# A decode block with adaptive layernorm, cached attention and a feed-forward layer: constant matmuls in the tail, and the last V tile ahead of the output weight

## The chip, the cores and the metric

The kernel runs on one core of one Trainium2 chip. The metric is the device time of one execution in microseconds; three plain runs of the kernel before gave 1332.01 to 1332.98 us, with a median of 1332.43.

## The reference

Four sequences decode one token each. D is 512, there are 32 heads of 128, the cache holds 4096 keys and values per head, all in f32 (k_cache and v_cache are 268 MB each).

```python
mod = (_silu(c) @ w_mod).reshape(c.shape[0], 6, 1, -1)
sa, ca, ga, sb, cb, gb = (mod[:, i] for i in range(6))
h = _layernorm(x) * (1 + ca) + sa
q = (h @ wq).reshape(B, Sq, H, Dh).transpose(0, 2, 1, 3)
p = softmax(einsum("bhqd,bhkd->bhqk", q, k_cache) * Dh ** -0.5)
o = einsum("bhqk,bhkd->bhqd", p, v_cache)
x = x + ga * (o.transpose(0, 2, 1, 3).reshape(B, Sq, H * Dh) @ wo)
h = _layernorm(x) * (1 + cb) + sb
x = x + gb * (_silu(h @ w1) @ w2)
```

## The kernel before

The attention is cut into N = 64 steps, one for each pair of heads (t, 16 of them) and sequence (b, 4). A step has a K tile and a V tile of 4 MiB each, 128 partitions of 32 KB. All large tiles (the modulation weights, wq, the K and V tiles, then the two halves of wo, w1 and w2) share one pool, `kv`, of five buffers: a load starts when the tile that had its buffer has been read for the last time. All these loads are issued by SyncE (SP in the profile), in the order of the program, and move in that order.

In a step, GpSimd multiplies 24 of the 64 rows of the K tile by the query, and VectorE the other 40 (`mult`, line 216); VectorE sums the products (`red`, 221) and takes each partition's maximum (`rowmax`, 225). TensorE transposes the maxima (`bmax`, 229), VectorE reduces them (`negmax`, 236), ScalarE computes the exponentials into a zero-padded tile (`softexp`, 247), and TensorE multiplies these with V in 16 matmuls of 512 columns (`pv`, 260), each against 32 columns of weights, so that four column groups work side by side. In f32 each matmul is two records in the trace.

Behind the four steps of a pair t, `finish_a` copies the accumulated rows and sums them with small matmuls (lines 269 to 277), and `finish_b` scales them into `oz`. `project(lo, hi)` (294) multiplies pairs lo to hi of `oz` with wo, 8 matmuls of 128 columns for each pair, into one accumulator, `accp`. The first half of wo (`wo0`) serves pairs 0 to 7, the second (`wo1`, in four pieces) pairs 8 to 15.

The tail, behind step 63, is one chain: `finish_a` and `finish_b` of the last pair, `project(NH, NT)`, the residual (345, 346), the second layernorm with two one-column matmuls (165, 169), a transpose, w1 (352, 16 matmuls of 448 columns in four groups k), SiLU (126, 127), a transpose, w2 (362, 56 matmuls of 128 columns), the last residual and four small stores. `project(0, NH)` stands on TensorE ahead of pv(63).

Scheduling is by hand: each engine runs its instructions in the order in which the program writes them. `psum("q", 2)` hands out two PSUM banks in turn, which make_qb (202) and, at the end, w1's product use. `qs` holds the scaled queries and `ident` the identity matrix; both stay unchanged to the end.

Of the kernel before, what the change touches and what calls it, by code (L numbers as in the profile page):

```python
# [17 lines left out]
def kernel(  # L18
# [13 lines left out]
    nc = tc.nc  # L32
    P = 128
    B, H, S, Dh = kc.shape
    D = x.shape[2]
# [3 lines left out]
    HP = 2  # L39
    HALF = P // HP  # L40
    NT = H // HP
# [4 lines left out]
    NI = F // P  # L46
# [4 lines left out]
    N = B * NT  # L51
# [8 lines left out]
    def psum(shape, tag, bufs):  # L60
        return ps.tile(shape, F32, tag=tag, name=tag, bufs=bufs)
# [3 lines left out]
    wov = wo.rearrange("(t p j) n -> p t j n", p=P, j=HP)  # L65
    w1v = w1.rearrange("(p k) f -> p k f", p=P)
    w2v = w2.rearrange("(p i) d -> p i d", p=P)

    def fetch(t, src, *cuts):
        for lo, hi in zip(cuts, cuts[1:]):  # L70
            nc.sync.dma_start(t[:, lo:hi], src[:, lo:hi])

    def load(name, shape, src, *cuts):
        t = kv.tile(shape, F32, tag="kv", name=name)
        fetch(t, src, *(cuts or (0, shape[1])))
        return t
# [3 lines left out]
    def load_k(n):  # L80
        t, b = divmod(n, B)
        src = kc[b, HP * t : HP * (t + 1)].rearrange("h (p j) d -> (h p) j d", p=HALF)
        kt[n] = load(f"k{n}", [P, NJ, Dh], src)

    def load_v(n):
        t, b = divmod(n, B)
        src = vc[b, HP * t : HP * (t + 1)].rearrange("h (p j) d -> (h p) j d", p=HALF)
        vt[n] = load(f"v{n}", [P, NJ, Dh], src)
# [14 lines left out]
    ident = const.tile([P, P], F32, name="ident")  # L103
# [25 lines left out]
    def transposed(src, m, name):  # L129
        d = const.tile([P, m, W], F32, name=name)  # L130
        nc.vector.transpose(d, src.rearrange("p (c k) -> p k c", k=m))  # L131
        return d
# [23 lines left out]
    def layernorm_mod(dst, src, sh, sc1):  # L156
        def t(tag, n):
            return work.tile([P, n], F32, tag=tag, name=tag, bufs=1)

        st, mv, dm, q, r, u = t("st", 6), t("mv", 2), t("dm", 1), t("lnq", 1), t("lnr", 2), t("lnu", P)  # L160
        nc.vector.bn_stats(st, src)
        nc.vector.bn_aggr(mv, st)
        avgm = avg.rearrange("p g w -> p (g w)")
        pm = psum([P, 1], "mx", 2)
        nc.tensor.matmul(pm, avgm, mv[:, 0:1], start=True, stop=True)
        nc.vector.tensor_sub(dm, mv[:, 0:1], pm)
        nc.vector.scalar_tensor_tensor(q, dm, dm, mv[:, 1:2], op0=ALU.mult, op1=ALU.add)
        pq = psum([P, 1], "mx", 2)
        nc.tensor.matmul(pq, avgm, q, start=True, stop=True)
        nc.vector.scalar_tensor_tensor(u, src, pm, sc1, op0=ALU.subtract, op1=ALU.mult)  # L170
        nc.scalar.activation(r[:, 0:1], pq, AF.Sqrt, bias=epst)
        nc.vector.reciprocal(r[:, 1:2], r[:, 0:1])
        nc.vector.scalar_tensor_tensor(dst, u, r[:, 1:2], sh, op0=ALU.mult, op1=ALU.add)
# [7 lines left out]
    CW = 4 * Dh  # L181
    pq = [psum([P, CW], "q", 2) for _ in range(2)]
    for k in range(NK):
        for ch in range(H * Dh // CW):
# [3 lines left out]
                start=k == 0, stop=k == NK - 1,  # L188
            )
    qs = const.tile([P, 2, CW], F32, name="qs")  # L190
# [5 lines left out]
    def make_qb(t):  # L196
        p = psum([P, B, Dh], "q", 2)
        for b in range(B):
            for i in range(HP):
                ch, u = divmod(HP * t + i, CW // Dh)  # L200
                j, g = divmod(ch, G)
                nc.tensor.matmul(  # L202
                    p[HALF * i : HALF * (i + 1), b, :],
                    ident[:, W * g + b : W * g + b + 1].to_broadcast([P, HALF]),
                    qs[:, j, u * Dh : (u + 1) * Dh],
                    start=True, stop=True,
                )
        qb[t] = p
        qw[t] = work.tile([P, B, Dh], F32, tag="qw", name=f"qw{t}")
        nc.scalar.activation(qw[t], p, AF.Copy)  # L210
# [3 lines left out]
    def mult(eng, src, n, lo, hi):  # L214
        t, b = divmod(n, B)
        eng.tensor_mul(  # L216
            kt[n][:, lo:hi, :], kt[n][:, lo:hi, :], src[t][:, b : b + 1, :].to_broadcast([P, hi - lo, Dh])
        )

    def red(n, lo, hi):  # L220
        nc.vector.tensor_reduce(sc[n][:, lo:hi], kt[n][:, lo:hi, :], axis=AX.X, op=ALU.add)  # L221

    def rowmax(n):
        nm[n] = work.tile([P, 1], F32, tag="rm", name=f"rm{n}", bufs=3)
        nc.vector.tensor_reduce(nm[n], sc[n], axis=AX.X, op=ALU.max)  # L225

    def bmax(n):
        p = psum([P, P], "mx", 2)
        nc.tensor.transpose(p, nm[n].to_broadcast([P, P]), ident)  # L229
        nm[n] = p  # L230

    def negmax(n):
        t = work.tile([P, 1], F32, tag="nm", name=f"nm{n}", bufs=3)
        for i in range(HP):
            h = slice(HALF * i, HALF * (i + 1))
            nc.vector.tensor_reduce(t[h], nm[n][h, h], axis=AX.X, op=ALU.max, negate=True)  # L236
        nm[n] = t
# [29 lines left out]
    def finish_a(t):  # L267
        o = work.tile([P, JJ, Dh], F32, tag="o", name="o")
        nc.vector.tensor_copy(o, po[t].rearrange("p (j d) -> p j d", j=JJ))  # L269
        d = psum([P, 1 + HP, B], "small", 1)  # L270
        nc.tensor.matmul(d[:, 0, :], blk, rs[t], start=True, stop=True)
        for i in range(HP):
            for r in range(HP):
                for j in range(JJ):
                    s = i * W // 2 + j
                    nc.tensor.matmul(  # L276
                        d[HALF * i : HALF * (i + 1), 1 + r, :], o[:, j, r::HP], sel[:, s : s + JJ * (B - 1) + 1 : JJ],
                        start=j == 0, stop=j == JJ - 1,
                    )
        sm[t] = d  # L280

    def finish_b(t):
        rd = work.tile([P, 1, B], F32, tag="rd", name="rd")
        nc.vector.reciprocal(rd, sm[t][:, 0:1, :])
        nc.vector.tensor_mul(oz[:, t, :, :B], sm[t][:, 1 : 1 + HP, :], rd.to_broadcast([P, HP, B]))  # L285

    accp = psum([P, P], "acc", 1)
    wot = []

    def project(lo, hi):  # L290
        for t in range(lo, hi):
            for r in range(HP):
                for g in range(G):
                    nc.tensor.matmul(  # L294
                        accp[W * g : W * (g + 1), :], oz[:, t, r, :],
                        wot[t // NH][:, t % NH, r, g * P : (g + 1) * P],
                        start=(t == 0 and r == 0), stop=(t == NT - 1 and r == HP - 1),
                    )

    NH = NT // 2  # L300
    make_qb(0)
    load_v(0)
    for n in range(N):
        t, b = divmod(n, B)
        if n + 1 < N - 3:
            load_k(n + 1)
            load_v(n + 1)
        elif n == N - 4:
            load_k(N - 3)
            load_k(N - 2)  # L310
            load_k(N - 1)
        elif n == N - 3:
            load_v(N - 3)
            load_v(N - 2)
        elif n == N - 2:
            wot.append(load("wo0", [P, NH, HP, D], wov[:, :NH]))
        else:
            load_v(n)
            wot.append(load("wo1", [P, NH, HP, D], wov[:, NH:], 0, NH // 2, 3 * NH // 4, NH - 1, NH))
        sc[n] = work.tile([P, NJ], F32, tag="sc", name=f"sc{n}", bufs=3)  # L320
        mult(nc.gpsimd, qw, n, 0, NA)
        mult(nc.vector, qb, n, NA, NJ)
        if n >= B and b == 0:
            finish_a(t - 1)
        red(n, NA, NJ)
        if n >= B and b == 0:
            finish_b(t - 1)
        red(n, 0, NA)
        rowmax(n)
        bmax(n)  # L330
        negmax(n)
        softexp(n)
        if n == N - 1:
            w1t = load("w1", [P, NK, F], w1v, 0, 2, 3, 4)
            w2t = load("w2", [P, NI, D], w2v, 0, 8, 12, 13, 14)
            project(0, NH)
        pv(n)
        if b == 1 and t + 1 < NT:
            make_qb(t + 1)
    finish_a(NT - 1)  # L340
    finish_b(NT - 1)
    project(NH, NT)

    x1 = const.tile([P, P], F32, name="x1")
    nc.vector.tensor_mul(x1, ga, accp)
    nc.vector.tensor_add(x1, x1, xg)
    layernorm_mod(hg, x1, sb, cb1)
    h2T = transposed(hg, NK, "h2T")
    ph = psum([P, FG], "q", 2)
    for k in range(NK):  # L350
        for g in range(G):
            nc.tensor.matmul(  # L352
                ph[W * g : W * (g + 1), :], h2T[:, k, :], w1t[:, k, g * FG : (g + 1) * FG],
                start=k == 0, stop=k == NK - 1,
            )
    hid = const.tile([P, FG], F32, name="hid")
    silu2(hid, ph, FG)
    hidT = transposed(hid, NI, "hidT")
    pf = psum([P, P], "po", 2)
    for i in range(NI):  # L360
        for g in range(G):
            nc.tensor.matmul(  # L362
                pf[W * g : W * (g + 1), :], hidT[:, i, :], w2t[:, i, g * P : (g + 1) * P],
                start=i == 0, stop=i == NI - 1,
# [32 lines left out]
```

## Time and profile before

| What | Value |
|---|---|
| Median of three plain runs | 1332.43 us |
| The profiled execution, in all | 1334.54 us |
| Its span, from the first to the last instruction | 1332.5 us |
| VectorE busy | 976.2 us (73%) |
| TensorE matmuls busy | 504.9 us (38%) |
| GpSimd, ScalarE busy | 435.2, 75.7 us |
| Bytes read from HBM | 567.30 MB, 426 GB/s over the span |
| Granted TensorE clock, mean | 0.656 of 2.4 GHz |

The DMA engines are busy to nine tenths or more in 39 of the span's 40 slices; no engine is. Busy shares are over the whole span, and say little about its last 4%, where the loads run out and the engines wait for each other. There the rows of the section below are read. The granted clock of a stretch is a mean of two levels, 0.5 (1.2 GHz) and 1.0 (2.4 GHz).

### The profile page before, as it was taken

Reading aid. Unit: us, or ns where it says so; the run is one execution under the profiler, and the core shown is the slowest. Engines: PE = TensorE matmul, PEld = TensorE weight load, DVE = VectorE, ACT = ScalarE, POOL = GpSimd, SP = SyncE. Lnnn points to the kernel's source line nnn. Section 1 sums busy time; section 2 is a strip of 40 time slices with the busy share of each in tenths; the row PEclk is TensorE's granted clock in tenths of the full one; section 3 lists DMA queues with packets and bytes.
Section 4 is the critical chain, followed back from the end, with each engine's and each line's share of the span. In section 5 each row is a group of like instructions: output and inputs, shape, how many; then the busy total and the mean of one; then the engine's idle time right before and its main releaser. Section 6 shows DMA issues by size and latency. Waiting matters only on the chain.

```text
span 1332.5 us, 8833 instructions
## 1 busy us (share of the span) xinstructions
PE 504.9 (38%) x3576; PEld 181.2 (14%) x3576; DVE 976.2 (73%) x468; ACT 75.7 (6%) x289; POOL 435.2 (33%) x79
## 2 busy tenths in 40 slices
PE   3244324433442533443343233334333333433157
PEld 2011101110110111101011110101111011101024
DVE  1487787788778778777877877777787787778851
ACT  1100000000000000000000000000000000000000
POOL 1244234324323423432442343243234234324600
PEclk9666677666656666656666676576666556666677
DMA  9999999999999999999999999999999999999997
GB/s 407 427 430 433 426 436 428 429 435 426 433 432 429 433 427 435 430 430 432 427 435 429 428 434 429 432 430 431 432 429 430 430 432 432 431 428 433 431 414 288
DMA packets 22376, 567.87 MB, mean 426 GB/s; under 512 B 2448, under 2 KB 2496, under 8 KB 5056
## 3 DMA queue, kind: packets, MB, share of 16 engines
q1 hardware_dynamic: 22160, 567.29, 99.3%
q8 instruction: 28, 0.46, 0.1%
q14 instruction: 12, 0.10, 0.0%
q0 software_dynamic: 128, 0.01, 0.0%
q10 hardware_dynamic: 48, 0.01, 0.0%
HBM read 567.30 MB, written 0.01 MB: 426 GB/s over the span
## 4 chain that ended last, share of the span: by engine, by line
DMA 48%; DVE 35%; PE 10%; issue 4%; ACT 2%; DVEq 0%; ACTq 0%
DMA k<-in_A_k_cache_dram 45%; DVE sc L221 20%; DVE k L216 13%; PE po L260 8%; DMA v<-in_A_v_cache_dram 2%; ACT pz L247 2%; PE mx L229 1%; DMA wm<-in_w_mod_dram 1%; DVE o L269 1%; DVE rm L225 1%; DVE nm L236 1%; PE acc L294 0%; PE po L362 0%; PE q L352 0%; DVE oz L285 0%
## 5 line engine op out<-in xcount | busy, mean ns | idle before, releaser
L216 POOL TENSOR_TENSOR k<-k,qw 128x3072 f32<-128x3072 f32 x64 | 429.7, 6715 | 827.9 <-DMA k<-in_A_k_cache_dram 786.7
L221 DVE TENSOR_REDUCE sc<-k 128x40 f32<-128x5120 f32 (+1 forms) x128 | 560.8, 4413 | 5.2
L216 DVE TENSOR_TENSOR k<-k,q 128x5120 f32<-128x5120 f32 x64 | 351.2, 5488 | 245.9 <-DMA k<-in_A_k_cache_dram 188.2
L260 PE MATMUL po<-v,pz 128*32 128x512 f32 x2048 | 371.5, 892 | 103.0 <-ACT pz L247 77.1
L229 PE MATMUL mx<-ident,rm 128*128 128x128 f32 x64 | 28.5, 445 | 641.4 <-DVE rm L225 641.4
L260 PEld LDWEIGHTS po<-v,pz 128*32 128x32 f32 x2048 | 82.6, 155 | 349.0 <-issue 256.3
L247 ACT ACTIVATE pz<-sc,nm 64x64 f32<-64x64 f32 x128 | 44.2, 345 | 1054.1 <-DVE nm L236 1052.5
L229 PEld LDWEIGHTS mx<-ident,rm 128*128 128x128 f32 x64 | 11.6, 181 | 676.2 <-issue 648.2
L236 DVE TENSOR_REDUCE nm<-mx 64x1 f32<-64x64 f32 x128 | 28.4, 222 | 45.9 <-PE mx L229 43.9
L276 PE MATMUL small<-sel,o 128*64 128x4 f32 x512 | 43.0, 231 | 46.6 <-DVE o L269 46.6
L276 PEld LDWEIGHTS small<-sel,o 128*64 128x64 f32 x512 | 41.6, 190 | 48.0 <-DVE o L269 48.0
L247 ACT ACTIVATION_READ_ACCUMULATOR pz<-sc,nm 64x1 f32 x128 | 23.6, 185 | 0.0
L269 DVE COPY o<-po 128x512 f32<-128x512 f32 x16 | 11.0, 684 | 16.2 <-PE po L260 16.2
L202 PE MATMUL q<-qs,ident 128*64 128x128 f32 x256 | 17.5, 279 | 0.0
L225 DVE TENSOR_REDUCE rm<-sc 128x1 f32<-128x64 f32 x64 | 14.1, 220 | 2.2
L202 PEld LDWEIGHTS q<-qs,ident 128*64 128x64 f32 x256 | 13.6, 136 | 14.5 <-issue 14.5
L210 ACT ACTIVATE qw<-q 128x512 f32<-128x512 f32 x16 | 9.6, 597 | 105.5 <-PE q L202 105.5
L146 PE MATMUL q<-wm,csT 128*32 128x128 f32 x192 | 7.5, 322 | 17.2 <-DVE csT L131 13.5
L186 PE MATMUL q<-wq,hT 128*32 128x512 f32 x64 | 10.1, 790 | 9.5 <-DMA wq<-in_A_wq_dram 9.5
L294 PE MATMUL acc<-wo,oz 128*32 128x128 f32 x256 | 11.7, 369 | 0.4 <-DMA wo<-in_A_wo_dram 0.4
L294 PEld LDWEIGHTS acc<-wo,oz 128*32 128x32 f32 x256 | 11.2, 154 | 0.7 <-issue 0.6
L146 PEld LDWEIGHTS q<-wm,csT 128*32 128x32 f32 x192 | 6.2, 129 | 17.9 <-DVE csT L131 13.5
(57 smaller groups left out, 63.8 us busy)
## 6 DMA issues: line engine op xcount, KB each, us to landing
k<-in_A_k_cache_dram SPq DMA_DIRECT2D x64, 4096.0 KB, 36.0
v<-in_A_v_cache_dram SPq DMA_DIRECT2D x64, 4096.0 KB, 30.3
wq<-in_A_wq_dram SPq DMA_DIRECT2D x2, 4096.0 KB
wm<-in_w_mod_dram SPq DMA_DIRECT2D x2, 3072.0 KB, 10.1
wo<-in_A_wo_dram SPq DMA_DIRECT2D x1, 4096.0 KB
wo<-in_A_wo_dram SPq DMA_DIRECT2D x1, 2048.0 KB
w<-in_B_w_dram SPq DMA_DIRECT2D x1, 2048.0 KB, 23.7
w<-in_B_w_dram SPq DMA_DIRECT2D x1, 1792.0 KB
```

What stands on the lines that cost most here:

```text
L146: nc.tensor.matmul(p[W * g : W * (g + 1), u, :], csT[:, k, :], wmt[k // 2][:, k % 2, o : o + P], start=k == 0, stop=k == NK - 1,)
L202: nc.tensor.matmul(p[HALF * i : HALF * (i + 1), b, :], ident[:, W * g + b : W * g + b + 1].to_broadcast([P, HALF]), qs[:, j, u * Dh : (u + ...
L216: eng.tensor_mul(kt[n][:, lo:hi, :], kt[n][:, lo:hi, :], src[t][:, b : b + 1, :].to_broadcast([P, hi - lo, Dh]))
L221: nc.vector.tensor_reduce(sc[n][:, lo:hi], kt[n][:, lo:hi, :], axis=AX.X, op=ALU.add)
L225: nc.vector.tensor_reduce(nm[n], sc[n], axis=AX.X, op=ALU.max)
L229: nc.tensor.transpose(p, nm[n].to_broadcast([P, P]), ident)
L236: nc.vector.tensor_reduce(t[h], nm[n][h, h], axis=AX.X, op=ALU.max, negate=True)
L247: nc.scalar.activation(w[:, :, o + i * W // 2 : o + i * W // 2 + JJ], sc[n][h].rearrange("p (g j) -> p g j", j=JJ), AF.Exp, bias=nm[n][h], ...
L260: nc.tensor.matmul(po[t][W * g : W * (g + 1), :], pz[n % NP][:, j * W + o : (j + 1) * W + o], vt[n][:, JJ * j : JJ * (j + 1), :].rearrange ...
L269: nc.vector.tensor_copy(o, po[t].rearrange("p (j d) -> p j d", j=JJ))
L276: nc.tensor.matmul(d[HALF * i : HALF * (i + 1), 1 + r, :], o[:, j, r::HP], sel[:, s : s + JJ * (B - 1) + 1 : JJ], start=j == 0, stop=j == ...
L294: nc.tensor.matmul(accp[W * g : W * (g + 1), :], oz[:, t, r, :], wot[t // NH][:, t % NH, r, g * P : (g + 1) * P], start=(t == 0 and r == 0 ...
```

## The change

`busy(m)` issues m matmuls of a constant: the identity against the first 512 columns of `qs`, into a PSUM bank that nothing reads. It is called at seven places: ten matmuls ahead of the transpose of step 63's maxima, five ahead of the second half of the projection, and 2, 3, 2, 2 and 4 in the tail, 28 in all. The V tile of step 63 is loaded ahead of wo0, which comes in two pieces; w2 comes in five pieces where it came in four. `project(0, NH)` moves behind pv(63), in two halves with `finish_a` between them, and pairs 8 to 14 are projected ahead of the last one.

```diff
+    idle = []
+
+    def busy(m):
+        if not idle:
+            idle.append(psum([P, CW], "q", 2))
+        for _ in range(m):
+            nc.tensor.matmul(idle[0], ident, qs[:, 0, :], start=True, stop=True)
+
     make_qb(0)
...
         elif n == N - 2:
-            wot.append(load("wo0", [P, NH, HP, D], wov[:, :NH]))
+            load_v(N - 1)
+            wot.append(load("wo0", [P, NH, HP, D], wov[:, :NH], 0, NH // 2, NH))
         else:
-            load_v(n)
             wot.append(load("wo1", [P, NH, HP, D], wov[:, NH:], 0, NH // 2, 3 * NH // 4, NH - 1, NH))
+            busy(10)
...
         if n == N - 1:
             w1t = load("w1", [P, NK, F], w1v, 0, 2, 3, 4)
-            w2t = load("w2", [P, NI, D], w2v, 0, 8, 12, 13, 14)
-            project(0, NH)
+            w2t = load("w2", [P, NI, D], w2v, 0, 4, 8, 11, 13, 14)
         pv(n)
         if b == 1 and t + 1 < NT:
             make_qb(t + 1)
+    project(0, NH // 2)
     finish_a(NT - 1)
+    project(NH // 2, NH)
+    busy(5)
+    project(NH, NT - 1)
     finish_b(NT - 1)
-    project(NH, NT)
+    project(NT - 1, NT)
...
     nc.vector.tensor_add(x1, x1, xg)
+    busy(2)
     layernorm_mod(hg, x1, sb, cb1)
     h2T = transposed(hg, NK, "h2T")
+    busy(3)
     ph = psum([P, FG], "q", 2)
...
                 start=k == 0, stop=k == NK - 1,
             )
+        if k in (1, 2):
+            busy(2)
+    busy(4)
     hid = const.tile([P, FG], F32, name="hid")
```

On TensorE, from pv(62) on to the first matmuls of the projection behind the last sums over heads (L229 is the transpose of step 63's maxima, L260 pv, L294 the projection, L271 and L276 the sums, L307 the constant):

```order
 L260 MATMUL po<-v_2922,pz_113 32x512 x16
-L229 MATMUL mx<-ident,rm_2998 128x128
-L294 MATMUL acc<-wo_2954,oz 32x128 x64
-L260 MATMUL po<-v_2986,pz_111 32x512 x16
+L307 MATMUL q<-qs,ident 128x512 x10
+L229 MATMUL mx<-ident,rm_3010 128x128
+L260 MATMUL po<-v_2954,pz_111 32x512 x16
+L294 MATMUL acc<-wo_2956,oz 32x128 x32
 L271 MATMUL small<-rs_2900,blk 128x4
 L276 MATMUL small<-sel,o 64x4 x16
-L294 MATMUL acc<-wo_2988,oz 32x128 x64
+L294 MATMUL acc<-wo_2956,oz 32x128 x32
```

The first half of the projection went from ahead of pv(63) to behind it, around the sums, and ten constants stand ahead of the transpose.

On TensorE, from the layernorm's second matmul (L169) to w2 (w1 is L352 before and L366 now, w2 L362 and L379):

```order
 L169 MATMUL mx<-lnq,avg 128x1
-L352 MATMUL q<-w_3007,h2T 32x448 x16
-L362 MATMUL po<-w_3011,hidT 32x128 x56
-L393 UNCONDITIONAL_BRANCH
+L307 MATMUL q<-qs,ident 128x512 x3
+L366 MATMUL q<-w_3019,h2T 32x448 x8
+L307 MATMUL q<-qs,ident 128x512 x2
+L366 MATMUL q<-w_3019,h2T 32x448 x4
+L307 MATMUL q<-qs,ident 128x512 x2
+L366 MATMUL q<-w_3019,h2T 32x448 x4
+L307 MATMUL q<-qs,ident 128x512 x4
+L379 MATMUL po<-w_3023,hidT 32x128 x56
```

w1's sixteen matmuls are parted by two pairs of constants, with three ahead of them and four behind.

On SyncE, the loads behind K of step 63, before (v_2920, v_2922 and v_2986 are the V tiles of steps 61 to 63, wo_2954 and wo_2988 are wo0 and wo1):

```order
L71 DMA v_2920<-in_A_v_cache_dram 128x8192
L71 DMA v_2922<-in_A_v_cache_dram 128x8192
L71 DMA wo_2954<-in_A_wo_dram 128x8x1024
L71 DMA v_2986<-in_A_v_cache_dram 128x8192
L71 DMA wo_2988<-in_A_wo_dram 128x4x1024
```

and now (v_2954 is step 63's, wo_2956 and wo_2989 are wo0 and wo1):

```order
L71 DMA v_2920<-in_A_v_cache_dram 128x8192
L71 DMA v_2922<-in_A_v_cache_dram 128x8192
L71 DMA v_2954<-in_A_v_cache_dram 128x8192
L71 DMA wo_2956<-in_A_wo_dram 128x4x1024 x2
L71 DMA wo_2989<-in_A_wo_dram 128x4x1024
```

The V tile of step 63 went one load forward, and wo0 is two loads.

## Rows read from the trace of the kernel before

**Rows 1.** Chain that ended last, from 1260 us: start us, us, what.

```profile
1267.96 30.29 DMA v<-in_A_v_cache_dram
...
1298.39 6.58 PE po L260 x32
...
1305.74 1.88 PE small L276 x32
1307.62 5.34 PE acc L294 x128
...
1314.29 0.37 PE mx L165 x2
...
1315.24 0.37 PE mx L169 x2
...
1316.96 4.96 PE q L352 x32
...
1324.16 4.97 PE po L362 x112
```

**Rows 2.** Timeline of SyncE's queue, single issues: start us, us, engine line op, count.

```profile
1252.23 0.39 SPq L71 DMA_DIRECT2D wo<-in_A_wo_dram  x1
...
1298.32 0.86 SPq L71 DMA_DIRECT2D w<-in_B_w_dram  x1
...
1303.37 0.33 SPq L71 DMA_DIRECT2D w<-in_B_w_dram  x1
...
1305.91 1.60 SPq L71 DMA_DIRECT2D w<-in_B_w_dram  x2
```

**Rows 3.** Timeline of TensorE: a step's pv, then steps 62 and 63 [idle before].

```profile
1235.64 5.49 PE L260 MATMUL po<-v,pz 128*32 128x512 f32 x32 [1.30 <-ACT pz L247]
...
1276.88 5.34 PE L260 MATMUL po<-v,pz 128*32 128x512 f32 x32 [4.38 <-DMA v<-in_A_v_cache_dram]
...
1287.79 0.44 PE L229 MATMUL mx<-ident,rm 128*128 128x128 f32 x1 [5.57 <-DVE rm L225]
...
1288.60 6.33 PE L294 MATMUL acc<-wo,oz 128*32 128x128 f32 x128 [0.37 <-DMA wo<-in_A_wo_dram]
```

**Rows 4.** Windows: from:to, us, PE busy, granted clock, DMA share, GB/s.

```profile
1280.44:1287.26 6.82, 1.78 (x19) 1.00 1.07 437
...
1297.50:1304.33 6.83, 5.94 (x29) 0.50 1.03 413
1304.33:1307.74 3.41, 2.91 (x50) 0.99 1.03 426
1307.74:1311.16 3.42, 3.42 (x72) 0.51 1.00 417
1311.16:1317.98 6.82, 3.48 (x80) 1.00 1.02 424
1317.98:1321.40 3.42, 3.42 (x24) 0.51 0.74 306
...
1324.81:1328.22 3.41, 3.41 (x72) 0.51 0.04 12
```

**Rows 5.** Weight loads and make_qb's matmuls, from the timeline, then two groups of loads.

```profile
1280.72 0.16 PEld L260 LDWEIGHTS po<-v,pz 128*32 128x32 f32 x4 [0.27 <-issue]
1281.15 0.16 PEld L260 LDWEIGHTS po<-v,pz 128*32 128x32 f32 x4 [0.27 <-issue]
...
1300.07 0.23 PEld L260 LDWEIGHTS po<-v,pz 128*32 128x32 f32 x4 [0.62 <-issue]
1300.92 0.23 PEld L260 LDWEIGHTS po<-v,pz 128*32 128x32 f32 x4 [0.62 <-issue]
...
1182.51 1.09 PE L202 MATMUL q<-qs,ident 128*64 128x128 f32 x16
...
L202 PEld LDWEIGHTS q<-qs,ident 128*64 128x64 f32 x256 | 13.6, 136 | 14.5 <-issue 14.5
L229 PEld LDWEIGHTS mx<-ident,rm 128*128 128x128 f32 x64 | 11.6, 181 | 676.2 <-issue 648.2
```

## The prediction

> **What bounds the kernel now.** I read the chain of waits first, because the change touches only the last 50 us. In that stretch the chain stands on one transfer and then on TensorE: v63 is issued at 1267.96 us and lands after 30.29 us, its matmuls take 6.58 us, then come the sums over heads (1.88), the second half of the output projection (5.34), the layernorm with two tiny matmuls, w1 (4.96 from 1316.96) and w2 (4.97 from 1324.16, so until 1329.13) [rows 1]. Next the DMA queue's own rows: a load is issued there when its buffer and its semaphore are free, so the four issues from 1298.32 on are also landing times: v63 at 1298.3, then the pieces of wo1 at 1303.4, 1305.9 and about 1307.2 (the last of the two rows that begin at 1305.91) [rows 2]. That is 2, 1 and 0.5 MiB in 5.05, 2.54 and about 1.3 us: 2.53 us a MiB, all the time. By that rate the last piece of wo1 lands at 1308.5, w1 (1.75, 0.875, 0.875 MiB) at 1312.9, 1315.1 and 1317.3, and w2 (3.5 MiB) at 1326.1. Nothing of this moves with the change: the same bytes stand in the same queue, only v63 and wo0 change places. So the reader should see two limits close together: w2's last landing, 1326.1, and TensorE's end, 1329.1. Last I read windows cut where the granted clock changes: TensorE works in long stretches at the lower level (1.2 GHz, share 0.5) in the tail: 1297.50 to 1304.33, 1307.74 to 1311.16, 1317.98 to 1321.40 and 1324.81 to 1328.22; it rises only behind a stretch of dense matmuls, and falls behind idle ones [rows 4].
>
> **v63 ahead of wo0.** In the kernel before, wo0 takes the buffer that k61 leaves at 1252.23 and v63 follows when k62 is done [rows 1, 2]. Now v63 has the first place. pv(62) starts on v62's landing at 1276.88 [rows 3]; 4 MiB at 2.53 us is 10.1, so v63 lands near 1287 instead of 1298.3, and wo0 (in halves) near 1292 and 1298. No issue gets later: the extra pieces wait for landings that come well before the queue reaches them.
>
> **The constant's price.** The trace has no such matmul. One is 128x512 in f32 against a full 128-column weight and should be two records, as each of the kernel's other f32 matmuls. The nearest rows are pv's: four column groups stream 512 columns side by side, and the next round's weights are loaded 0.85 us after the last at the lower level and 0.43 at the upper one (2.4 GHz) [rows 5]. So one constant matmul is 2 x 0.427 = 0.85 us at the upper level, 1.71 at the lower. The bound above adds its weight loads, if no stream hides them: 181 ns each in the row of a 128-wide load. I take them as hidden: make_qb's 16 records, eight in each half of the columns, take 1.09 us with loads of 136 ns, where loads in the open would make it 8 x (0.107 + 0.136) = 1.9 [rows 5]. The Trainium skill speaks against it: "TensorE: Matmul & The Clock Gate", Part 3, section "The mechanism", says that a weight load overlaps matmuls in flight only in another row group, and the constant always has all rows. make_qb's loads have all rows too and overlap, so this trace doesn't bear the rule out; by it each constant matmul would cost 0.36 us more.
>
> **The sum.** At the upper level throughout, I rescale each burst by the stretches it lay in (time at the lower level, plus twice that at the upper, halved) [rows 1, 4]: pv 5.94 low + 0.64 high gives 3.6; project's 64 matmuls 3.42 low + 1.92 high gives 3.6; w1 3.42 + 1.54 gives 3.25; w2 3.41 + 1.57 gives 3.3. Now step by step:
> - pv(62) ends at 1282.2, at the upper level since 1280.44 [rows 3, 4]. Ten constants, 8.5 us, until 1290.8. They lie in TensorE's wait for the row maximum, which was over at 1287.79 [rows 3]: the transpose behind them is 3 us late, and so are the exponentials. That would matter if v63 were not also early. Transpose 0.35, then 1.30 for maximum and exponentials [rows 3]: pv(63) starts at 1292.4, 6.0 earlier than before; v63 has landed. It ends at 1296.0.
> - project(0, 4) 1.8 (before, all of project(0, 8) lay hidden in the wait for v63, 6.33 us from 1288.60 [rows 3]; it is now on the path), which hides the copy of po; sums over heads 2.2 with the denominators; project(4, 8) 1.8: 1301.8. Five constants 4.3: 1306.1. They delay little, since the last of wo1 lands at 1308.5. project(8, 15) 3.2, project(15, 16) 0.45: the accumulator is ready at 1309.7, where it was 1312.96. So far -3.2 us.
> - Two constants (1.7) against the wait for the statistics (1312.96 to 1314.29, 1.33) [rows 1]: 0.4 late. The two tiny matmuls 1.3: 1312.75. Three constants (2.6) against the rest of the layernorm (1315.61 to 1316.96, 1.35): 1.2 late, w1 starts at 1315.3.
> - w1 3.25, with four constants between its parts, 3.4: it ends at 1322.0, as before (1321.92). Without them it would have waited for w1's last landing at 1317.3 and ended near 1318.5: the constants take this gain.
> - Four constants (3.4) against SiLU and transpose (1321.92 to 1324.16, 2.24): 1.2 late, w2 starts at 1325.4. At the upper level it takes 3.3 instead of 4.97: 1328.65, where it was 1329.13.
> The sum is -3.2 + 0.4 + 1.2 - 1.7 + 3.4 + 1.2 - 1.7, about **-0.5 us**. VectorE's last steps and the stores stay as they are. Against the profiled execution's own 1334.54 us that is 1334.0; the plain runs have a median of 1332.43, 2.1 lower, so I forecast 1331.9.
>
> What hides what: the five constants lie under wo1's landings; if wo1 came sooner they would cost 4.3. All later ones lie partly open, and pay only because the clock stays up: the upper level is worth 3.4 us on w1 and w2 together, and the constants behind the accumulator cost about 6.2.
>
> **The rivals.**
> 1. The constants are hidden and the transfers bound. Floor: w2's last piece at 1326.1 and four matmuls, 0.2: -2.8 us, 1329.6. For it: everything up to the accumulator runs into landings. Against: 13 constants stand behind it, 11 us of TensorE in 18. Chance 0.08. More than this can't be won while the queue is full.
> 2. The clock falls all the same, somewhere from pv(63) to w2, since small matmuls and waits stand between the constants. One such stretch in the tail lasts 3.4 to 6.8 us [rows 4], and each us in it at the lower level gives half a us back: 1.7 to 3.4 us, 1333.6 to 1335.3. For it: the copy and the sums over heads took the clock down before (up from 1304.33, low at 1307.74, with 1.88 us of 4-column matmuls) [rows 1, 4]. Against: dense matmuls now stand right before and behind. One long stretch decides for slower; a short one does not. Chance 0.10. If a constant didn't raise the clock at all, all 18 behind pv(63) would cost twice as much, 15 us more; that is within this chance, at 0.01.
> 3. The weight loads lie open. Then 56 loads (28 constants of two records) at 0.136 to 0.181 us [rows 5] add 7.6 to 10.1 us, less 1 that wo1's landings cover: 1338.5 to 1341. It turns to slower from 0.06 us a load on. Against: make_qb. Chance 0.04.
> 4. My own: no change that can be told, chance 0.78. Inside it lies the case that before differs from its profile: that execution had four low stretches in the tail, others may have fewer, and a change that repairs the clock then gains nothing and costs up to 1 us.
>
> **How the numbers follow.** I count 0.2%, 2.7 us, as what can be told from no change. Rival 1 ends at -2.8, on that line, so half of it is faster, and a few hundredths I keep for landings other than worked out: faster 0.08. Slower: rival 3 and two thirds of rival 2, 0.11. Same: 0.81. The range goes down to rival 1 (1329.6) and up into the short end of rival 2 (1334.2); it leaves out the long low stretch and rival 3.
>
> **What would show it.** Right: v63's matmuls start on ScalarE's exponentials, not on a DMA, near 1292.4; the L307 records start 0.43 us apart at the upper level; the accumulator is ready near 1309.7 with waits for wo1 gone or short; granted clock 1.0 from 1294 on; w1 ends near 1322 and w2 takes 3.3 us from behind the last constant. Wrong: records 0.56 us or more apart (rival 3), a stretch at 0.5 behind pv(63) (rival 2), w2 waiting for its DMA (rival 1), or transfers that end at another time than 1326.

## The result: 0.23% slower, and the profile after

Nine runs of the changed kernel, the profiled one among them, have a median of 1335.66 us (1334.57 to 1336.62); nine of the kernel before, 1332.51 (1331.86 to 1333.43). The ratio is 1.0023, 95% interval 1.0014 to 1.0032: 3.15 us slower, where I forecast 0.5 us faster and a range up to 1334.2. The profiled execution took 1336.26 us, with a span of 1334.4.

The chain of waits of the changed kernel, from step 62's matmuls on (start us, us, what; lines 307, 366 and 379 are the constant, w1 and w2):

```profile
1276.79 6.40 PE po L260 x32
1283.18 8.78 PE q L307 x20
1291.96 0.12 PE mx L229
...
1293.38 3.64 PE po L260 x32
1297.02 1.75 PE acc L294 x64
...
1299.08 1.81 PE small L276 x32
1300.89 1.88 PE acc L294 x64
1302.77 4.49 PE q L307 x10
1307.26 3.63 PE acc L294 x128
1310.89 1.91 PE q L307 x4
...
1313.51 0.35 PE mx L169 x2
1313.87 2.68 PE q L307 x6
1316.55 1.64 PE q L366 x16
1318.19 1.91 PE q L307 x4
1320.10 0.89 PE q L366 x8
1320.99 1.91 PE q L307 x4
1322.91 0.89 PE q L366 x8
1323.80 3.63 PE q L307 x8
1327.43 3.24 PE po L379 x112
```

From 1276.79 on no transfer is in this chain: each piece of TensorE's work ends where the next begins, but for the steps at 1292 and 1313 that VectorE and ScalarE take. Before, the same stretch began with a wait for v63 until 1298.3 [rows 1]. Now pv(63) starts at 1293.38, 5 us earlier, and w2 still ends 1.5 us later than in the first profile of before: 1330.67 against 1329.13.

The windows of the changed kernel on TensorE (from:to, us, PE busy, granted clock, DMA share, GB/s) answer to [rows 4]:

```profile
1290.00:1300.00 10.00, 8.70 (x124) 1.00 1.03 411
1300.00:1310.00 10.00, 10.00 (x196) 1.00 1.02 418
1310.00:1320.00 10.00, 9.41 (x69) 1.00 0.99 404
1320.00:1330.70 10.70, 10.62 (x141) 1.00 0.24 97
```

The constants do what they can do: the clock stands at the upper level (2.4 GHz) in every window to the end, where before it fell four times. In the last three, 30.7 us, TensorE idles for 0.7. The transfers end in the last window; its DMA share is 0.24. Their times are those worked out: the SyncE queue's issues behind wo1's landings, single rows of the timeline, stand at

```profile
1302.91 0.33 SPq L71 DMA_DIRECT2D w<-in_B_w_dram  x1
1305.53 0.33 SPq L71 DMA_DIRECT2D w<-in_B_w_dram  x1
1306.81 0.33 SPq L71 DMA_DIRECT2D w<-in_B_w_dram  x1
1308.08 0.33 SPq L71 DMA_DIRECT2D w<-in_B_w_dram  x1
```

which is within half a microsecond of before [rows 2]. The projection's second half began at 1307.26, so the five constants ahead of it covered wo1 almost to the end, as the sum had it. They cover more than that: the accumulator is ready at 1310.89, where in traces below that wait for wo1 it is ready at 1308.8 (twice the constants in w1) and 1309.2 (none at all).

### The profile page after: what moved, and what is told of

Read it like the earlier page. It is cut to its first block, busy times and chain, and to the rows that moved or that the text cites. A ratio compares the mean times of both kernels' runs of the same rounds, so it can differ in the third digit from the quotient of the medians.

```text
span 1334.4 us, 8947 instructions
## 1 busy us (share of the span) xinstructions
PE 520.8 (39%) x3632; PEld 185.3 (14%) x3632; DVE 976.2 (73%) x468; ACT 75.7 (6%) x289; POOL 435.1 (33%) x79
## 4 chain that ended last, share of the span: by engine, by line
DMA 46%; DVE 35%; PE 12%; issue 5%; ACT 2%; DVEq 0%; ACTq 0%
DMA k<-in_A_k_cache_dram 43%; DVE sc L221 20%; DVE k L216 13%; PE po L260 8%; DMA v<-in_A_v_cache_dram 3%; ACT pz L247 2%; PE q L307 2%; PE mx L229 1%; DMA wm<-in_w_mod_dram 1%; DVE o L269 1%; PE acc L294 1%; DVE rm L225 1%; DVE nm L236 1%; PE q L366 0%; PE po L379 0%
## 5 line engine op out<-in xcount | busy, mean ns | idle before, releaser
L260 PE MATMUL po<-v,pz 128*32 128x512 f32 x2048 | 369.3, 887 | 99.8 <-ACT pz L247 78.4
L229 PE MATMUL mx<-ident,rm 128*128 128x128 f32 x64 | 28.3, 443 | 638.2 <-DVE rm L225 638.2
L260 PEld LDWEIGHTS po<-v,pz 128*32 128x32 f32 x2048 | 82.0, 155 | 344.8 <-issue 250.2
L229 PEld LDWEIGHTS mx<-ident,rm 128*128 128x128 f32 x64 | 11.5, 180 | 672.4 <-issue 643.6
L276 PE MATMUL small<-sel,o 128*64 128x4 f32 x512 | 42.3, 230 | 46.8 <-DVE o L269 46.8
L276 PEld LDWEIGHTS small<-sel,o 128*64 128x64 f32 x512 | 40.9, 187 | 48.1 <-DVE o L269 48.1
L307 PE MATMUL q<-qs,ident 128*128 128x512 f32 x56 | 25.9, 605 | 0.0
L202 PE MATMUL q<-qs,ident 128*64 128x128 f32 x256 | 17.5, 279 | 0.0
L307 PEld LDWEIGHTS q<-qs,ident 128*128 128x128 f32 x56 | 10.1, 190 | 13.6 <-issue 13.6
```

The costliest lines, as they stand in the source:

```text
L202: nc.tensor.matmul(p[HALF * i : HALF * (i + 1), b, :], ident[:, W * g + b : W * g + b + 1].to_broadcast([P, HALF]), qs[:, j, u * Dh : (u + ...
L260: nc.tensor.matmul(po[t][W * g : W * (g + 1), :], pz[n % NP][:, j * W + o : (j + 1) * W + o], vt[n][:, JJ * j : JJ * (j + 1), :].rearrange ...
L276: nc.tensor.matmul(d[HALF * i : HALF * (i + 1), 1 + r, :], o[:, j, r::HP], sel[:, s : s + JJ * (B - 1) + 1 : JJ], start=j == 0, stop=j == ...
L307: nc.tensor.matmul(idle[0], ident, qs[:, 0, :], start=True, stop=True)
```

## The experiments

Theory A: behind pv(63) the changed kernel is bound by TensorE, which is at the upper level anyhow, and the 18 constants there cost more than the level gives back; without them the transfers bound. Its rivals: B, the lower level would take the same time without constants; C, the new order is what costs; D, the constants in w1 are hidden; and for the part of the price that the sum did not have, S and E below.

**No constants.** The calls of `busy` go, all else stays.

```diff
-            busy(10)
...
-    busy(5)
...
-        if k in (1, 2):
-            busy(2)
-    busy(4)
```

> The changed kernel without any of its 28 constants: v63 still ahead of wo0, the projection still in its new order. Theory A (behind pv(63) the changed kernel is bound by TensorE at the upper level without a gap, and the 18 constants there cost more than the clock pays back): TensorE waits again for wo1 (last piece near 1308) and w2 (near 1326), the end of w2's matmuls goes from 1330.7 to 1326 or 1327, so 3.5 to 4.5 us less than the changed kernel: 1331.1 to 1332.2 us. Rival B (without constants the lower level takes the same time back): 1334 or more, with w1 and w2 at the lower level on the path. Rival C (the new order of loads and of the projection is what costs): 1335 or more, whatever the clock does.

Measured: 1332.03 us (1331.77 to 1332.17, 11 runs), ratio to before 0.9993 (0.9984 to 1.0002). 3.6 us less than the changed kernel, as A said; B and C fall. Its chain:

```profile
1288.25 20.16 DMA wo<-in_A_wo_dram
1308.55 0.68 PE acc L294 x16
...
1313.22 5.96 PE q L354 x32
...
1321.44 4.98 PE po L364 x112
```

The transfers are back in it: the accumulator ends on wo1's last piece, at 1309.2, 1.7 us earlier than with constants. w1 then runs almost wholly and w2 mostly at the lower level (5.96 and 4.98 us), and w2 still ends at 1326.4. The windows of this run, columns as above:

```profile
1310.00:1320.00 10.00, 6.62 (x36) 0.66 0.98 404
1320.00:1326.40 6.40, 4.94 (x112) 0.73 0.41 162
```

TensorE is busy for 4.94 of w2's 4.98 us, so w2 itself does not wait for a transfer here. But its last piece, issued at 1308.43, lands 17.5 us later, at 1325.9: the upper level has at most half a us left to win. Where w2 does run at it, in the kernel without constants inside w1 below, it waits for its landings and ends at 1326.49.

**Constants only.** The kernel before, with the same constants at the same places:

```diff
+            busy(10)
...
     finish_a(NT - 1)
+    busy(5)
     finish_b(NT - 1)
     project(NH, NT)
```

and the calls in the tail as in the change.

> The kernel before with the constants alone: the loads, their pieces and the projection as before; 10, 5, 2, 3, 2, 2 and 4 constants at the same places of the program. Theory A: pv(63) waits for v63 until 1298.4; then pv 3.6, sums 3.0, five constants 4.5 and the second half of the projection 3.7 make the accumulator ready at 1313.1, and from there the tail of the changed kernel takes 19.8 us: 2.2 us later than it, 1337 to 1339 us. Rival C (the order costs, the constants are about free): 1331 to 1333.

Measured: 1339.45 us (5 runs, 1337.79 to 1342.35), ratio 1.0054 (1.0041 to 1.0068): slower than either, against C. It is a little over the range of A, since in the profiled execution step 63's matmuls, behind a wait for v63, took 5.37 us and not 3.6:

```profile
1268.01 30.02 DMA v<-in_A_v_cache_dram
...
1298.17 5.37 PE po L260 x32
...
1310.67 3.63 PE acc L294 x128
1314.31 1.91 PE q L307 x4
```

So the two parts of the change go opposite ways: with the constants, the early v63 and the moved projection save 3.8 us (1339.45 to 1335.66); without them they save what noise covers.

**No constants behind the projection.** The first 15 stay, the 13 of the tail go:

```diff
-    busy(2)
...
-    busy(3)
...
-        if k in (1, 2):
-            busy(2)
-    busy(4)
```

> The changed kernel with its first 15 constants (10 ahead of the transpose, 5 ahead of the projection's second half) and without the 13 behind the projection. Theory A: the accumulator is ready at 1310.9 as in the changed kernel; layernorm 4, w1 behind its last landing (1317.1) near 1318, w2 bound by its own landings, 1326: 3.5 to 4.5 us less than the changed kernel, 1331.1 to 1332.2, the same as without any constant. Rival B: the level falls in the layernorm and w1 and w2 give 2 to 3 us back: 1333.5 to 1335.

Measured: 1332.21 us (11 runs), ratio 0.9997 (0.9988 to 1.0006). The median is A's. But the profiled execution took 1334.13, and there the windows of TensorE show the low stretches that B speaks of:

```profile
1313.70:1320.50 6.80, 5.43 (x30) 0.50 0.96 390
1320.50:1323.90 3.40, 1.09 (x24) 1.00 0.57 231
1323.90:1327.30 3.40, 3.40 (x72) 0.50 0.11 41
```

Almost all of w1 and most of w2 lay at 0.50. One other run of the eleven was at 1333.91, the rest between 1331.97 and 1332.54. The lower level alone does not make these 2 us: with no constants at all w1 and w2 took as long (5.96 and 4.98 us), in an execution of 1331.94. The starts differ:

```profile
1307.65 3.67 PE acc L294 x128
...
1315.50 5.70 PE q L364 x32
...
1323.46 4.97 PE po L374 x112
```

Here the accumulator is ready at 1311.32, behind a pv(62) of 6.53 us and fifteen constants; there it was ready at 1309.22, on wo1's landing. So by these two traces the lower level in w1 and w2 costs some 2 us where the accumulator is late, and at most half a us where it is not. That the short runs of this kernel are of the second kind fits their times, but no trace of one is on record.

**No constants inside w1, and twice as many.** Two kernels that change one line:

```diff
         if k in (1, 2):
-            busy(2)
+            busy(4)
```

and the same without the two lines.

> The changed kernel without the two pairs of constants between the parts of w1. Theory A: these stand open, since w1's pieces have landed 3 us before TensorE comes to them; both bursts of 1.91 us go, w1 ends at 1320.0, w2 starts behind the last four constants at 1323.6 and ends near 1326.9: 3.8 us less, 1331.9. Rival D (they lie in the wait for w1's landings and cost little): 1335 or more.

> The changed kernel with 4 and 4 constants between the parts of w1 where it has 2 and 2. Theory A: four more constants of 0.854 us, with no more changes from one kind of matmul to another: 3.4 us more, 1339.1. Rival D: less than 1 us more.

Measured: without 1332.37 us (10 runs, ratio 0.9996, 0.9987 to 1.0006), with twice as many 1338.63 (4 runs, ratio 1.0043, 1.0029 to 1.0056). From none to two to four in each place: 1332.4, 1335.7, 1338.6. The second step is the columns of four constants (3.4 expected, 3.0 measured), the first stops on the transfers; the chain without them ends

```profile
1306.81 18.52 DMA w<-in_B_w_dram
...
1325.37 0.65 PE po L377 x16
...
1326.02 0.47 PE po L377 x8
```

on w2's landings, at 1326.49. D falls: these four constants, 3.8 us in the chain after, stand open, and taking them out alone undoes the loss. All three kernels with fewer constants (1332.03, 1332.21 and 1332.37) come down to about the same time. So they show that the constants put TensorE's work behind the transfers, and not what each set costs by itself.

**Narrow constants.** Each constant in four pieces of 32 weight columns, as the kernel's own large matmuls are; the same columns stream, since four run side by side.

```diff
-            nc.tensor.matmul(idle[0], ident, qs[:, 0, :], start=True, stop=True)
+            for g in range(G):
+                nc.tensor.matmul(
+                    idle[0][W * g : W * (g + 1), :], ident[:, W * g : W * (g + 1)], qs[:, 0, :], start=True, stop=True
+                )
```

> The changed kernel with each constant matmul cut into four of 32 columns of weights, one for each column group, as pv, projection, w1 and w2 are: the same columns streamed, the same PSUM rows written. Each burst of constants takes some 0.2 us more than 0.854 us a constant in the changed kernel. Theory S (that is the price of going from 32-column tiles to a 128-column tile and back): the six bursts behind pv(63) give back 1 to 1.5 us, 1334.2 to 1334.7. Rival E (every burst has its own end of 0.1 to 0.2 us, whatever the tile): within 0.4 us of 1335.7.

Measured: 1333.88 us (11 runs, ratio 1.0011, 1.0002 to 1.0020), 1.8 us less than the changed kernel: S, a little beyond its range, and not E. The intervals of the two ratios overlap, so the chains have to decide: from the end of pv(62) to the end of w2 it is 45.98 us here and 47.49 in the changed kernel. The chain, with line 308 the constant, 369 w1 and 382 w2:

```profile
1282.19 8.58 PE q L308 x80
...
1306.01 3.49 PE acc L294 x128
1309.51 1.72 PE q L308 x16
...
1318.41 0.75 PE q L369 x8
...
1321.63 3.43 PE q L308 x32
1325.07 3.10 PE po L382 x112
```

Two constants take 1.72 us, twice 0.86, where 128 wide they took 1.91; and the kernel's own work behind them is faster too, 0.75 for 0.89 in w1 and 3.10 for 3.24 in w2. Each change from one tile width to the other cost 0.14 to 0.2 us. "TensorEngine Tiling (Array Packing)" of the Trainium skill, section "Key Properties", says that a change of tiling mode, other than a change of tile, drains TensorE; these rows agree with that, and show its price, though not the drain itself.

**Before, twice more.** The kernel before, unchanged, profiled again.

> The kernel before once more, for a second profile. If its tail depends on where the stretches of the lower level happen to fall, this execution has them elsewhere and w2's matmuls end anywhere from 1326.5 to 1329.2 (it was 1329.1), with the whole time moving along. If the 2.1 us between the profiled execution and the plain runs are the profile's own, the end is again within 0.5 us of 1329.1.

> The kernel before once more, for a third profile of its tail. If its time moves with the place of the low stretches and is cut off below by the transfers: w2's matmuls end between 1326.2 and 1329.2, the more the longer the low stretches on pv(63), w1 and w2.

Measured: 1332.38 and 1332.22 us, one run each. The ends of the two chains, of the second profile

```profile
1297.87 23.93 DMA w<-in_B_w_dram
...
1321.93 5.05 PE po L362 x112
```

and of the third:

```profile
1298.02 23.80 DMA w<-in_B_w_dram
...
1321.95 4.96 PE po L362 x112
```

w2 ends at 1326.98 and 1326.91, 2.2 us before the 1329.13 of the first profile [rows 1], and in both it has waited for the landing of its first piece, 8 of 14. There w1 began at 1313.04 and 1313.98, where the first profile has 1316.96. The clock had stood at the upper level through more of the work ahead; the second profile's timeline shows step 63 and the projection at their upper durations, with a wait for wo1 behind:

```profile
1297.94 3.64 PE L260 MATMUL po<-v,pz 128*32 128x512 f32 x32 [1.73 <-DMA v<-in_A_v_cache_dram]
...
1308.35 0.65 PE L294 MATMUL acc<-wo,oz 128*32 128x128 f32 x16 [0.71 <-DMA wo<-in_A_wo_dram]
```

v63 landed within 0.45 us in all three profiles, so most of the 2.2 us lies in the level that step 63 and the projection met; and since these two profiled executions took no longer than the plain runs, the profile adds no fixed time of its own. That the plain runs differ for the same reason is likely but not shown, since their tails are not on record. The 21 plain runs of before beside the first four experiments reach from 1331.80 to 1334.34, the 21 beside the other four from 1331.93 to 1334.59; their lower end is where the kernel without constants always is, and the first profiled execution, 1334.54, stands at their upper end.

## Why the prediction was wrong

- **The step that failed** is "two limits close together: w2's last landing, 1326.1, and TensorE's end, 1329.1". The second was not a limit of the kernel but the end of one execution: two more profiles have it at 1326.98 and 1326.91, where w2 waits for its transfer already. The forecast shortened that one end, and took the 2.1 us by which this execution lay above the plain runs for a fixed amount to take off again. Set against the other two ends, the sum's own 1328.65 is 1.7 us slower. Rival 4 named this case, at "up to 1 us". So there were at most 0.5 to 1 us to win (1332.03 without constants against medians of 1332.51 and 1333.07, a difference that noise covers), and not 2.8.
- **The constant's price** was mis-sized in one term. A record in a stream is what the sum had: ten constants in 8.78 us are 0.88 each. Their loads lie hidden, as taken; two of them in the timeline of the changed kernel's weight loads:

```profile
1284.08 0.19 PEld L307 LDWEIGHTS q<-qs,ident 128*128 128x128 f32 x1 [0.24 <-issue]
1284.51 0.19 PEld L307 LDWEIGHTS q<-qs,ident 128*128 128x128 f32 x1 [0.24 <-issue]
```

  one 128-column load of 0.19 us each 0.43, without a gap between the matmuls. So rival 3 did not come. The sentence of the Trainium skill's "TensorE: Matmul & The Clock Gate", Part 3, "The mechanism", that a load overlaps matmuls in flight only in another row group does not hold here; the same section also lets a load into the background weight buffer run ahead, which these rows allow. What the sum lacked is the change of tile width, 0.14 to 0.2 us each time. From the end of pv(62) to the end of w2 it had 46.45 us; the trace has 47.49, and 45.98 with narrow constants. So the width is 1.5 us, of which some 0.5 was made up elsewhere: with narrow constants w1 and w2 took 3.00 and 3.10 us, where the sum had 3.25 and 3.3.
- **The start** was 1.0 us late: pv(62) took 6.40 us and not 5.34, with more of it at the lower level. That part goes with the execution: it took 5.34 us with narrow constants, 6.53 without those in the tail, and 3.64 with twice the constants in w1.
- **The account**: 2.2 (before's profile) + 1.0 (tile width, less what was made up) + 1.0 (pv(62)) is 4.2; the profiled execution after lay 0.6 above its own median, which leaves 3.6, and the forecast was off by 3.65 (from -0.5 to +3.15).
- **What held**: v63's wait went and step 63 started on the exponentials; wo1's landings covered the five constants in part, and wholly only where pv(62) was short; the four constants in w1 took what the early accumulator gave; w2 took 3.24 us at the upper level; rival 2, a low stretch behind pv(63), did not come in the profiled execution; and rival 1's floor, 1326.1, is where the kernels without the open constants end (1326.4, 1326.5). The reading that the level falls behind idle stretches has one exception in [rows 4], which rival 2 does use: TensorE was busy for 2.91 of 3.41 us from 1304.33 to 1307.74, and the level fell behind it.

## What to carry to other kernels

Before a wait is filled with work that keeps the clock up, find what else ends there: a transfer that lands no earlier takes the gain, and the filler itself can become the chain. Profile the kernel before more than once, and look whether its plain runs lie below the profiled one; a tail whose length follows the place of the low clock stretches needs a lower bound, not one profile's end. If a filler is needed, give it the tile width of the work beside it.

## What the runs showed of the hardware that I had not expected

A change between 128-column and 32-column tiles costs 0.14 to 0.2 us each way, in the constants' bursts (1.91 against 1.72 us) and in the work behind them (0.89 against 0.75). And the same kernel's tail differs by 2.2 us between profiles, with v63's landing within 0.45 us and the granted clock low in other places, while the kernel without constants, whose accumulator ends on wo1's landing, hardly varies: 0.4 us over eleven runs, against 2.5 us over 21 of before.
